# Pooled attention and a SiLU feed-forward on one core: attention of the next batch spread between the matmuls of each token tile

## The chip, the cores and the metric

The kernel runs on one core of one Trainium2 chip. The metric is the device time of one execution in microseconds (us); lower is better. The core has a matrix engine (PE, with its weight loads as PEld), a vector engine (DVE), ScalarE (ACT), GpSimd (POOL) and SyncE (SP); SP and POOL issue the DMAs of this kernel. SBUF is the on-chip memory, PSUM the memory that PE writes, used here in banks of 512 float32 columns.

## The reference

```python
def _attn_ref(q, k, v):                      # 8 batches, 8 heads, 576 positions, head dim 64
    pool = 8
    scale = 1.0 / np.sqrt(D)
    k_p = k.reshape(B, H, Sp, pool, D).mean(axis=3)       # Sp = 72
    v_p = v.reshape(B, H, Sp, pool, D).mean(axis=3)
    scores = scale * np.matmul(q, k_p.transpose(0, 1, 3, 2))
    scores = scores - np.max(scores, axis=-1, keepdims=True)
    attn = np.exp(scores)
    attn = attn / (np.sum(attn, axis=-1, keepdims=True) + 1e-09)
    return np.matmul(attn, v_p)

x = attn_out.transpose(0, 2, 1, 3).reshape(B * S, H * D)  # 4608 tokens x 512
h = x @ w_in                                              # 512 x 2048
g = h * (1.0 / (1.0 + np.exp(-h)))
out = g @ w_out                                           # 2048 x 512
```

Inputs and output are float32. Keys and values are averaged in groups of eight, so each query looks at 72 keys. A batch holds 576 tokens; 4608 tokens are nine tiles of 512.

## The kernel before, in words

The order of the instructions on each engine is made by a scheduler from the program, which is written as two loops one after the other.

**Attention** (`attn_head_pair`, 32 calls, one for each two heads of a batch). SP loads k and v of one head at a time (L121, L123, 144 KB each) into the tile `kvraw`, of which there are six. DVE adds up the groups of eight (L125, L130), makes a bf16 copy of v with a 65th column that holds 8.0 (L134, L135). PE transposes the pooled keys (L139) and the queries (L157, L160), which POOL loads with a cast to bf16 (L147, L151); ScalarE copies both out of PSUM (L141, L163). For each head PE makes the scores in a chunk of 512 and one of 64 queries (`sc_ps`, L170), ScalarE takes the exponential (`esT`, L177), PE multiplies by the values (`nu_ps`, L181: 64 rows of numerators, and the denominator as the 65th), ScalarE copies the result out (`numer_sb`, L184). SP writes the numerators to `x_pre_T` in HBM, transposed, and POOL writes the denominators to `denom_buf` (L186, L190).

**Feed-forward** (`moe_token_tile`, nine calls, one for each 512 tokens). SP reads `x_sb` (512 features x 512 tokens) and the denominators back (L200, L203). DVE takes the reciprocal (L205), POOL casts it (L207), PE spreads it to 64 rows for each head by a matmul with a table of zeros and ones (`rb_ps`, four for each tile, L211), and DVE multiplies x by it (L212). Then the "up" half: 16 groups of 4 matmuls of 512 columns into `hp_ps` (L218), each group followed by a Silu on ScalarE into `h_T` (L224). Then the "down" half: 4 groups of 16 matmuls into `o_ps` (L230), each copied out by ScalarE (L237) and stored by SP (L238). One tile has 128 of these large matmuls.

The weights `w_in` and `w_out` are loaded at the start by POOL with a cast to bf16, in one DMA each (L105, L107), ahead of its first load of q.

Of the kernel before, what the change touches and what calls it, by code (L numbers as in the profile page):

```python
# [27 lines left out]
FP32 = mybir.dt.float32  # L28
# [8 lines left out]
def kernel(  # L37
# [9 lines left out]
    nc = tc.nc  # L47
# [3 lines left out]
    Sp = S // POOL  # L51
    BH = B * H
# [3 lines left out]
    assert H % 2 == 0  # L56

    score_scale = float(1.0 / (D ** 0.5) / POOL)

    x_pre_T = nc.dram_tensor("x_pre_T", (d_model, NTOK), BF16, kind="Internal").ap()  # L60
    denom_d = nc.dram_tensor("denom_buf", (H, NTOK), BF16, kind="Internal").ap()

    k_pool = k.rearrange("b h (sp p) d -> b h sp p d", p=POOL)
    v_pool = v.rearrange("b h (sp p) d -> b h sp p d", p=POOL)

    S_CHUNKS = []
    s0 = 0
    while s0 < S:
        sl = min(512, S - s0)
        S_CHUNKS.append((s0, sl))  # L70
        s0 += sl
    QN = (S + 127) // 128
    NQ_FULL = QN - 1
    TL = S - 128 * NQ_FULL

# [3 lines left out]
    NT = NTOK // NTT  # L79

    w_in_r = moe_w_in.rearrange("(kt kp) f -> kp kt f", kp=128)
    w_out_r = moe_w_out.rearrange("(kt kp) d -> kp kt d", kp=128)
    xpt_r = x_pre_T.rearrange("(kt kp) t -> kp kt t", kp=128)

    singles = ctx.enter_context(tc.tile_pool(name="singles", bufs=1))
    ident = singles.tile([128, 128], FP32)
    make_identity(nc, ident)
    ident_bf = singles.tile([128, 128], BF16)
    nc.gpsimd.tensor_copy(out=ident_bf, in_=ident)

    trans_f = singles.tile([H, KF, 128], FP32, name="trans_f", bufs=1)
    nc.gpsimd.memset(trans_f, 1.0)
    nc.gpsimd.affine_select(
        out=trans_f, in_=trans_f, compare_op=ALU.is_ge, fill=0.0,
        base=0, channel_multiplier=-64, pattern=[[128, KF], [1, 128]],
    )
    nc.gpsimd.affine_select(
        out=trans_f, in_=trans_f, compare_op=ALU.is_ge, fill=0.0,
        base=63, channel_multiplier=64, pattern=[[-128, KF], [-1, 128]],
    )  # L100
    trans = singles.tile([H, KF, 128], BF16, name="trans", bufs=1)
    nc.gpsimd.tensor_copy(out=trans, in_=trans_f)

    w_in_sb = singles.tile([128, KF, d_ff], BF16)
    nc.gpsimd.dma_start(out=w_in_sb, in_=w_in_r)  # L105
    w_out_sb = singles.tile([128, KG, d_model], BF16)
    nc.gpsimd.dma_start(out=w_out_sb, in_=w_out_r)  # L107

    pools = {}

    def attn_head_pair(j):
        pa, pb, ps = pools["pa"], pools["pb"], pools["ps"]
        b = (2 * j) // H
# [168 lines left out]
```

## Time and profile before

| what | value |
|---|---|
| runs | 478.78, 475.38, 478.78 us; median 478.78 |
| profiled execution: span of the core | 476.0 us |
| busy in the span: PE, PEld, DVE, ACT, POOL | 374.4, 161.7, 189.2, 218.3, 127.2 us |
| instructions | 5267 |
| HBM read, written | 41.49 MB, 14.23 MB |
| DMA queues: issued by SP (hardware), by POOL (software) | 37.84 MB, 9.00 MB |

The profile is of one execution. Its span runs from the first to the last instruction, and is the profiled execution's own time; the runs were timed apart from it. In the rows of groups stand: line, engine, operation, output and inputs by the names of the program, shapes, count, then busy time and the mean duration of one in ns, then the idle time of the engine just before them and what ended it. In the timeline rows stand start (us), length (us), engine, line and operation; several of one kind in a row are merged ("x14"), and the length runs from the start of the first to the end of the last. Matmuls are pipelined: the length of one is longer than the distance to the next. In the rows by window stand the window, its length, then busy time and count for PE, PEld, DVE, ACT and POOL, the granted PE clock, the busy share of the DMA engines, and GB/s.

### The profile page before, as it was taken

The numbers are of one execution on the slowest core, as the hardware profiler recorded it, in microseconds if no ns is written. First come the engines' busy times: TensorE is split into PE (matmuls) and PEld (weight loads), VectorE is DVE, ScalarE is ACT, GpSimd is POOL, SyncE is SP. The second block draws the span as 40 slices with busy tenths as digits, with TensorE's granted clock in tenths as the row PEclk, the third lists the DMA queues.
The fourth block names the chain that finished last, engine by engine and source line by source line (L and its number), as shares of the span: only waits on it lengthen the run. The fifth ranks groups of instructions, "written<-read, shape, count | busy, mean of one in ns | idle before, by whom it ended". The sixth has DMA issues, their size and how long they took to land.

```text
span 476.0 us, 5267 instructions
## 1 busy us (share of the span) xinstructions
PE 374.4 (79%) x1612; PEld 161.7 (34%) x1636; DVE 189.2 (40%) x301; ACT 218.3 (46%) x502; POOL 127.2 (27%) x214
## 2 busy tenths in 40 slices
PE   0003777687777655379999999999999999999996
PEld 0001333233233321124444343443434434344342
DVE  5598766667766778999000202002020020200200
ACT  1002768778777665335162451623416244172441
POOL 7004878898699711210000000000000000000000
PEclk9999999999999999999999999999999999999999
DMA  7999999999999944321102112021120210201101
GB/s 174 239 228 199 155 146 158 157 172 162 157 158 176 162 147 136 84 81 44 67 22 90 44 44 90 1 90 44 49 85 0 90 44 14 75 0 45 45 22 67
DMA packets 69533, 47.18 MB, mean 99 GB/s; under 512 B 44344, under 2 KB 55168, under 8 KB 69504
## 3 DMA queue, kind: packets, MB, share of 16 engines
q1 hardware_dynamic: 25952, 37.84, 25.3%
q0 software_dynamic: 43552, 9.00, 21.0%
q8 instruction: 13, 0.21, 0.2%
q14 instruction: 16, 0.13, 0.1%
HBM read 41.49 MB, written 14.23 MB: 117 GB/s over the span
## 4 chain that ended last, share of the span: by engine, by line
PE 60%; DMA 17%; POOL 11%; issue 6%; ACT 3%; DVE 3%; SPq 0%; POOLq 0%; ACTq 0%
PE hp_ps L218 27%; PE o_ps L230 26%; DMA q_full<-in_q_dram 13%; POOL q_full L147 4%; POOL q_tail L151 3%; POOL denom_buf L190 3%; PE nu_ps L181 2%; PE rb_ps L211 2%; PE sc_ps L170 1%; ACT numer_sb L184 1%; DMA q_tail<-in_q_dram 1%; ACT esT L177 1%; DMA v_raw<-in_v_dram 1%; DMA x_sb<-x_pre_T 1%; PE qT_ps L157 1%
## 5 line engine op out<-in xcount | busy, mean ns | idle before, releaser
L218 PE MATMUL hp_ps<-x_sb,w_in_sb 128*128 128x512 bf16 x564 | 128.8, 384 | 1.7 <-ACT h_T L224 0.6
L230 PE MATMUL o_ps<-w_out_sb,h_T 128*128 128x512 bf16 x564 | 125.0, 379 | 0.6
L224 ACT ACTIVATE h_T<-hp_ps 128x512 bf16<-128x512 f32 x144 | 83.9, 597 | 52.8 <-PE hp_ps L218 52.7
L212 DVE TENSOR_TENSOR x_sb<-x_sb,rb_ps 128x512 bf16<-128x512 bf16 x36 | 23.0, 678 | 200.9 <-PE rb_ps L211 199.6
L218 PEld LDWEIGHTS <-w_in_sb 128*128 128x128 bf16 x576 | 55.6, 99 | 78.1 <-issue 15.3
L230 PEld LDWEIGHTS <-h_T 128*128 128x128 bf16 x576 | 56.4, 98 | 68.0
L130 DVE TENSOR_REDUCE v_p<-v_raw 72x64 f32<-72x512 f32 x64 | 64.6, 1010 | 22.2 <-DMA v_raw<-in_v_dram 20.1
L125 DVE TENSOR_REDUCE k_p_pair<-k_raw 72x64 f32<-72x512 f32 x64 | 64.7, 1011 | 19.3 <-DMA k_raw<-in_k_dram 18.9
L237 ACT COPY o_sb<-o_ps 128x512 f32<-128x512 f32 x36 | 21.1, 586 | 103.5 <-PE o_ps L230 97.7
L184 ACT CAST numer_sb<-nu_ps 65x512 bf16<-65x512 f32 (+1 forms) x128 | 44.3, 396 | 27.8 <-PE nu_ps L181 27.4
L147 POOL DMA_DIRECT2D q_full<-in_q_dram x64 | 52.9, 827 | 13.7 <-DMA w_in_sb<-in_moe_w_in_dram 11.3
L181 PE MATMUL nu_ps<-esT,vp_aug 72*65 72x512 bf16 (+1 forms) x128 | 41.8, 429 | 18.1 <-ACT esT L177 17.7
L177 ACT ACTIVATE esT<-sc_ps 72x512 bf16<-72x512 f32 (+1 forms) x128 | 45.1, 402 | 7.8 <-PE sc_ps L170 5.8
L170 PE MATMUL sc_ps<-q_T,kpT 64*72 64x512 bf16 (+1 forms) x128 | 44.2, 447 | 3.2 <-ACT kpT L141 2.4
L139 PE MATMUL kpT_ps<-ident,k_p_pair 72*128 72x72 f32 x32 | 11.7, 364 | 41.9 <-DVE k_p_pair L125 41.2
L190 POOL DMA_DIRECT2D denom_buf<-numer_sb x64 | 33.5, 524 | 40.7 <-ACT numer_sb L184 34.4
L151 POOL DMA_DIRECT2D q_tail<-in_q_dram x64 | 36.3, 567 | 20.6 <-DMA w_out_sb<-in_moe_w_out_dram 19.4
L207 POOL CAST recip_bf<-recip 8x512 bf16<-8x512 f32 x9 | 5.4, 603 | 124.4 <-PE rb_ps L211 112.0
L157 PE MATMUL qT_ps<-ident_bf,q_full 128*128 128x128 bf16 x128 | 20.5, 303 | 21.2 <-DMA q_full<-in_q_dram 16.2
L205 DVE RECIPROCAL recip<-den_sb 8x512 f32<-8x512 bf16 x9 | 29.4, 3305 | 0.0
L163 ACT COPY q_T<-qT_ps 128x576 bf16<-128x576 bf16 x32 | 20.4, 638 | 12.9 <-PE qT_ps L160 12.8
L181 PEld LDWEIGHTS <-vp_aug 72*65 72x65 bf16 x128 | 16.9, 148 | 26.9 <-issue 24.0
(25 smaller groups left out, 90.2 us busy)
## 6 DMA issues: line engine op xcount, KB each, us to landing
k_raw<-in_k_dram SPq DMA_DIRECT2D x64, 144.0 KB
v_raw<-in_v_dram SPq DMA_DIRECT2D x64, 144.0 KB
out_dram<-o_sb SPq DMA_DIRECT2D x36, 256.0 KB
x_pre_T<-numer_sb SPq DMA_DIRECT2D x64, 72.0 KB
x_sb<-x_pre_T SPq DMA_DIRECT2D x9, 512.0 KB
q_full<-in_q_dram POOLq DMA_DIRECT2D x64, 64.0 KB, 3.7
w_in_sb<-in_moe_w_in_dram POOLq DMA_DIRECT2D x1, 2048.0 KB, 17.5
w_out_sb<-in_moe_w_out_dram POOLq DMA_DIRECT2D x1, 2048.0 KB, 36.2
```

Of the source, the lines that this page charges most:

```text
L125: nc.vector.reduce_sum(out=k_p_pair[:, i, :], in_=k_raw.rearrange("a b c -> a c b"), axis=AX,)
L130: nc.vector.reduce_sum(out=v_p, in_=v_raw.rearrange("a b c -> a c b"), axis=AX)
L147: nc.gpsimd.dma_start(out=q_full[:, :, i, :], in_=q[b, h, : 128 * NQ_FULL, :].rearrange("(n p) d -> p n d", p=128),)
L151: nc.gpsimd.dma_start(out=q_tail[:TL, i, :], in_=q[b, h, 128 * NQ_FULL :, :],)
L170: nc.tensor.matmul(sc_ps[:, :sl], kpT[i * D : (i + 1) * D, :], q_T[i * D : (i + 1) * D, s0 : s0 + sl], start=True, stop=True,)
L177: nc.scalar.activation(esT[:, :sl], sc_ps[:, :sl], func=AF.Exp, scale=score_scale)
L181: nc.tensor.matmul(nu_ps[:, :sl], vp_augs[i], esT[:, :sl], start=True, stop=True)
L184: nc.scalar.copy(numer_sb[:, s0 : s0 + sl], nu_ps[:, :sl])
L190: nc.gpsimd.dma_start(out=denom_d[h : h + 1, tok0 : tok0 + S], in_=numer_sb[D : D + 1, :],)
L218: nc.tensor.matmul(hp_ps, w_in_sb[:, kk, gg * 128 : (gg + 1) * 128], x_sb[:, kk, :], start=(kk == 0), stop=(kk == KF - 1),)
L224: nc.scalar.activation(h_T[:, gg, :], hp_ps, func=AF.Silu)
L230: nc.tensor.matmul(o_ps, h_T[:, kk, mtok : mtok + 128], w_out_sb[:, kk, :], start=(kk == 0), stop=(kk == KG - 1),)
```

## The change

The kernel's body is written anew, and its order on each engine is the order in which it is written (`manual_schedule`); no scheduler moves anything.

- All of x, transposed, stays in SBUF (`xT`, 512 features x 4608 tokens, bf16). The tensors `x_pre_T` and `denom_buf` in HBM are gone, and so are `rb_ps` and its table.
- k, q and v of a whole batch come in one DMA each, all issued by SP in float32 (the first batch in two parts). POOL casts q to bf16; DVE pools k and v by three tensor-tensor additions each, in place of one reduction for each head.
- Two heads are worked on together. The scores of the two use the upper and the lower 64 rows of the PE array (`scores`), into two PSUM banks, and one Exp of 576 columns covers both. Denominators (against a block of ones that holds 8.0) and numerators of the two use the left and the right 64 columns (`values`), into one bank each. In the built program these matmuls have tiles of 64 x 128 and 128 x 64; all others have 128 x 128. Queries are taken in two halves of 288.
- 1/denominator is exp(-ln(denominator)) on ScalarE; DVE multiplies the numerators by it straight into `xT`. Ln and Exp lie in one activation table and Silu in another; the tables are loaded by hand, twice a tile.
- The batch a = t + 1 is worked on inside token tile t: `spread` calls a filler after a given matmul of the tile. In the up half: the loads of batch a + 1, the cast and the pooling, the transposes of k after matmul 22 and those of q after matmuls 26, 32, 38 and 44. In the down half: eight steps (four head pairs, two query halves), the scores after matmul 6n + 1 and the values after matmul 6n + 6. Batch 0 is worked on before the first tile; the last two tiles have no fillers.
- Large matmul outputs and transposes share three PSUM banks ("mm"). `o_ps` is copied out by DVE.
- The weights are loaded in four DMAs each, which POOL issues after its casts of the first q.

```diff
+    def load_batch(b, parts):
...
+        for i in range(parts):
+            hs = slice(i * hp, (i + 1) * hp)
+            nc.sync.dma_start(out=k_raw[:, hs, :], in_=k_src[:, hs, :])
+            nc.sync.dma_start(out=q_raw[:, hs, :], in_=q_src[:, hs, :])
+        for i in range(parts):
+            hs = slice(i * hp, (i + 1) * hp)
+            nc.sync.dma_start(out=v_raw[:, hs, :], in_=v_src[:, hs, :])
...
+    def pool_kv(b, which, parts):
...
+            w = POOL * D // 2
+            while w > D:
+                nc.vector.tensor_add(
+                    out=raw[:, hs, :w], in0=raw[:, hs, :w], in1=raw[:, hs, w : 2 * w]
+                )
+                w //= 2
+            nc.vector.tensor_add(
+                out=dst[:, hs, :], in0=raw[:, hs, :D], in1=raw[:, hs, D : 2 * D]
+            )
...
+    def q_transpose(b, p):
+        st = batches[b]
+        qT_ps = psum.tile([128, QJ, QP], BF16, tag="mm", bufs=3, name="qT_ps")
+        for j in range(QJ):
+            nc.tensor.transpose(
+                qT_ps[:, j, :],
+                st["q_bf"][:, p, j, :, :].rearrange("q s d -> q (s d)"),
+                ident[:QP, :QP],
+            )
+        qT = mid.tile([128, S], BF16, tag=f"qT{p}", bufs=1, name="qT")
+        nc.vector.tensor_copy(out=qT, in_=qT_ps.rearrange("d j q -> d (j q)"))
...
+    def scores(b, p, f):
+        st = batches[b]
+        cols = slice(f * HS, (f + 1) * HS)
+        sc_ps = psum.tile([SP, 2, 512], FP32, tag="sc", bufs=1, name="sc_ps")
+        for s in range(2):
+            rows = slice(s * D, (s + 1) * D)
+            nc.tensor.matmul(
+                sc_ps[:, s, :HS],
+                lhsT=st["kT"][rows, p, :],
+                rhs=st[f"qT{p}"][rows, cols],
+                start=True, stop=True,
+            )
+        es = mid.tile([SP, 2, HS], BF16, tag="es", bufs=3, name="es")
+        nc.scalar.activation(es, sc_ps[:, :, :HS], func=AF.Exp, scale=score_scale)
...
+    def values(b, p, f):
...
+        nu_ps = psum.tile([128, 512], FP32, tag="nd", bufs=3, name="nu_ps")
+        den_ps = psum.tile([128, 512], FP32, tag="nd", bufs=3, name="den_ps")
+        for s in range(2):
+            nc.tensor.matmul(
+                den_ps[s * D : (s + 1) * D, :HS],
+                lhsT=ones, rhs=es[:, s, :], start=True, stop=True,
+            )
+        for s in range(2):
+            nc.tensor.matmul(
+                nu_ps[s * D : (s + 1) * D, :HS],
+                lhsT=st["vp"][:, 2 * p + s, :], rhs=es[:, s, :],
+                start=True, stop=True,
+            )
+        lnd = mid.tile([128, HS], FP32, tag="lnd", name="lnd")
+        nc.scalar.activation(lnd, den_ps[:, :HS], func=AF.Ln)
+        rec = mid.tile([128, HS], FP32, tag="rec", name="rec")
+        nc.scalar.activation(rec, lnd, func=AF.Exp, scale=-1.0)
...
+    def spread(fillers, n):
+        todo = sorted(fillers, key=lambda f: f[0])
+        for i in range(n):
+            yield i
+            while todo and todo[0][0] <= i:
+                todo.pop(0)[1]()
...
+    for t in range(NT):
+        a = t + 1
+        f_up, f_down = [], []
+        if a < B:
+            if a + 1 < B:
+                f_up.append((0, lambda: load_batch(a + 1, 1)))
+            f_up.append((0, lambda: cast_q(a, 1)))
+            f_up.append((0, lambda: pool_kv(a, "k", 1)))
+            f_up.append((22, lambda: k_transpose(a)))
+            for p in range(NP):
+                f_up.append((26 + 6 * p, lambda p=p: q_transpose(a, p)))
+            f_up.append((50, lambda: pool_kv(a, "v", 1)))
+            f_down.append((0, attn_tables))
+            for n, (p, f) in enumerate(seq):
+                f_down.append((6 * n + 1, lambda p=p, f=f: scores(a, p, f)))
+                f_down.append((6 * n + 6, lambda p=p, f=f: values(a, p, f)))
+        moe_tables()
+        h_T = up(t, f_up)
+        down(t, h_T, f_down)
```

Where the instructions now stand, at three places. First, ScalarE between the last steps of attention and the first token tiles. Before, with `esT` the exponentials, `numer_sb` the copies out and `h_T` the Silus:

```order
L177 ACTIVATE esT<-sc_ps 72x64
L184 CAST numer_sb<-nu_ps 65x512
L184 CAST numer_sb<-nu_ps 65x64
L224 ACT_TABLE_LOAD
L224 ACTIVATE h_T<-hp_ps 128x512 x16
L237 COPY o_sb<-o_ps 128x512 x4
```
After, in each filled tile (`es` the exponentials, `lnd` and `rec` the two halves of the reciprocal):

```order
L211 ACT_TABLE_LOAD
L237 ACTIVATE h_T<-hp_ps 128x512 x16
L208 ACT_TABLE_LOAD
L177 ACTIVATE es<-sc_ps 72x576
L197 ACTIVATE lnd<-den_ps 128x288
L199 ACTIVATE rec<-lnd 128x288
```
The last three stand eight times in a row before the next table load; the copies of `o_ps` are no longer on this engine, and the tables change twice a tile.

Second, PE among the large matmuls. Before, where the down half of one tile ends and the next tile begins:

```order
L230 LDWEIGHTS h_T
L230 MATMUL o_ps<-w_out_sb,h_T 128x512
L211 LDWEIGHTS trans
L211 MATMUL rb_ps<-recip_bf,trans 128x512
...
L218 LDWEIGHTS w_in_sb
L218 MATMUL hp_ps<-x_sb,w_in_sb 128x512
```
After, in the first step of a down half (`sc_ps` the scores, `den_ps` and `nu_ps` denominators and numerators; rows that only repeat are left out at the dots):

```order
L250 MATMUL o_ps<-w_out_sb,h_T 128x512
L170 LDWEIGHTS kT
L170 MATMUL sc_ps<-qT,kT 72x288
...
L250 MATMUL o_ps<-w_out_sb,h_T 128x512
L186 LDWEIGHTS ones
L186 MATMUL den_ps<-es,ones 64x288
...
L191 LDWEIGHTS vp
L191 MATMUL nu_ps<-es,vp 64x288
...
L250 LDWEIGHTS h_T
L250 MATMUL o_ps<-w_out_sb,h_T 128x512
```
Scores and values have moved from a stage of their own to between the large matmuls.

Third, POOL at the start of the program. Before:

```order
L105 DMA w_in_sb<-in_moe_w_in_dram 128x4x2048
L102 CAST trans<-trans_f 8x512
L107 DMA w_out_sb<-in_moe_w_out_dram 128x16x512
L147 DMA q_full<-in_q_dram 128x4x64
L151 DMA q_tail<-in_q_dram 64x64
```
After:

```order
masks.py:199 AFFINE_SELECT ident<-ident 128x128
L267 MEMSET ones 72x64
L113 CAST q_bf<-q_raw 96x6x64 x8
L272 DMA w_in_sb<-in_moe_w_in_dram 128x4x512 x4
L275 DMA w_out_sb<-in_moe_w_out_dram 128x4x512 x4
L113 CAST q_bf<-q_raw 96x6x64 x56
```
The eight casts of the first q, which wait for its load, now stand ahead of the weights.

More of the change, by code (lines that the diff above doesn't have):

```diff
@@ L55 @@
     d_ff = moe_w_in.shape[1]
[L56 to L74, printed above, removed]
+    NP = H // 2
     KF = d_model // 128
@@ L195, in moe_token_tile @@
[L195 to L216 removed]
+    big = ctx.enter_context(tc.tile_pool(name="big", bufs=2))
```

263 lines of the change are left out of this document (126 added, 137 removed).

## Prediction

> **What bounds the kernel now.** I read the slices first, then the chain of waits, then busy time by stage.
>
> ```profile
> PE   0003777687777655379999999999999999999996
> ACT  1002768778777665335162451623416244172441
> PEclk9999999999999999999999999999999999999999
> DMA  7999999999999944321102112021120210201101
> PE 60%; DMA 17%; POOL 11%; issue 6%; ACT 3%; DVE 3%; SPq 0%; POOLq 0%; ACTq 0%
> ```
> ```profile
> 0.00:198.00 198.00, 111.26 (x448) 47.21 (x449) 142.33 (x258) 112.00 (x321) 122.32 (x206) 1.00 0.91 166
> 198.00:476.00 278.00, 263.15 (x1164) 114.53 (x1187) 46.83 (x44) 106.32 (x181) 4.83 (x8) 1.00 0.15 52
> ```
> There are two programs, one after the other. For 198 us (busy columns: PE, PEld, DVE, ACT, POOL) attention runs, its DMA engines full (share 0.91) and PE busy 111 of 198 us. Then for 278 us the token tiles run on PE alone, with DMA at 0.15. Neither uses what the other needs; the chain has DMA and POOL steps in the first part and little but matmuls in the second.
>
> The second part's rate, from the output copies (one per 16 matmuls, four per tile):
>
> ```profile
> 254.66 0.59 ACT L237 COPY o_sb<-o_ps 128x512 f32<-128x512 f32 x1 [2.90 <-PE o_ps L230]
> 258.12 0.59 ACT L237 COPY o_sb<-o_ps 128x512 f32<-128x512 f32 x1 [2.87 <-PE o_ps L230]
> 284.29 0.59 ACT L237 COPY o_sb<-o_ps 128x512 f32<-128x512 f32 x1 [2.90 <-PE o_ps L230]
> 472.37 0.59 ACT L237 COPY o_sb<-o_ps 128x512 f32<-128x512 f32 x1 [2.87 <-PE o_ps L230]
> ```
> A 512-column matmul takes 3.46/16 = 0.216 us. A tile takes 284.29 − 254.66 = 29.6 us; its 128 matmuls are 27.65, so some 2.0 belong to the four rb_ps broadcasts and their wait. The last copy starts 3.6 us before the end of the span (476.0).
>
> PE has a second speed, which the granted clock (9 throughout) does not show:
>
> ```profile
> 206.04 0.15 PEld L218 LDWEIGHTS <-w_in_sb 128*128 128x128 bf16 x1 [0.28 <-issue]
> 206.47 0.15 PEld L218 LDWEIGHTS <-w_in_sb 128*128 128x128 bf16 x1 [0.28 <-issue]
> 209.88 0.15 PEld L218 LDWEIGHTS <-w_in_sb 128*128 128x128 bf16 x1 [0.28 <-issue]
> L170 PE MATMUL sc_ps<-q_T,kpT 64*72 64x512 bf16 x64 | 40.8, 637 | 3.2 <-ACT kpT L141 2.4 <-ACT q_T L163 0.7
> L218 PE MATMUL hp_ps<-x_sb,w_in_sb 128*128 128x512 bf16 x564 | 128.8, 384 | 1.7 <-ACT h_T L224 0.6 <-DMA x_sb<-x_pre_T 0.3 <-issue 0.2
> ```
> The first token-tile matmuls come 0.43 us apart until 209.88, about 10 of them, and only then 0.216. All of attention runs at the slow rate (637 ns for 512 columns against 384).
>
> **The change, part by part.** *Removed:* the attention stage as a stage of its own, the rb_ps broadcasts (9 × 2.0 = 18 us), and the trip of x through HBM. Floor: nine tiles of 27.65 = 248.8 us. All that is added has to be paid per tile, at the start, or at the end.
>
> *Up half of a tile (seven tiles have attention to fill in).* 64 matmuls are 13.8 us. Between them stand 28 transposes, 4 of k and 24 of q:
>
> ```profile
> 86.58 0.58 PE L157 MATMUL qT_ps<-ident_bf,q_full 128*128 128x128 bf16 x4 [2.11 <-DMA q_full<-in_q_dram]
> L157 PE MATMUL qT_ps<-ident_bf,q_full 128*128 128x128 bf16 x128 | 20.5, 303 | 21.2 <-DMA q_full<-in_q_dram 16.2 <-DMA q_tail<-in_q_dram 2.9 <-DMA denom_buf<-numer_sb 2.0
> 6.50 0.35 PE L139 MATMUL kpT_ps<-ident,k_p_pair 72*128 72x72 f32 x1 [6.50 <-DVE k_p_pair L125]
> 6.89 0.22 ACT L141 CAST kpT<-kpT_ps 128x72 bf16<-128x72 f32 x1 [4.80 <-PE kpT_ps L139]
> L212 DVE TENSOR_TENSOR x_sb<-x_sb,rb_ps 128x512 bf16<-128x512 bf16 x36 | 23.0, 678 | 200.9 <-PE rb_ps L211 199.6 <-DMA x_sb<-x_pre_T 0.5
> L224 ACT ACTIVATE h_T<-hp_ps 128x512 bf16<-128x512 f32 x144 | 83.9, 597 | 52.8 <-PE hp_ps L218 52.7
> L207 POOL CAST recip_bf<-recip 8x512 bf16<-8x512 f32 x9 | 5.4, 603 | 124.4 <-PE rb_ps L211 112.0 <-DVE recip L205 12.3
> ```
> Four take 0.58 us, the last of them 0.3, so about 0.1 each at the slow rate; 96 columns at 0.216 per 512 would be 0.04. I take 0.08: 2.2 us (1.1 to 3.0). Stalls: DVE copies the last o_sb (0.68 by the tensor-tensor row), then pools k, 3584 elements a partition, 4.7 us at 678/512; so kp stands ready 5.6 us into the tile, and its transposes are due after 23 matmuls, 5.0. The transposes also take turns in the three "mm" banks: twice a bank comes back after four matmuls (0.86) while the Silu needs 1.03 (0.38 to the matmul's end, 0.6 for itself, and 0.05 for the hand-over, as from 6.85 to 6.89). Together 0.8. The eight q casts (0.5 each by POOL's 603 ns for 512) run in the tile before and hide; pooling v has some 3 us of slack. Up half: 16.8 us.
>
> *Down half.* 64 matmuls, 13.8, and eight steps, one after every six matmuls: two score matmuls, two for den_ps, two for nu_ps, each 288 columns, 0.121 us by 0.216 × 288/512. No row shows two half-array matmuls in different halves. Bounds for a pair: 0.12 (wholly side by side) and 0.24 (in turn). I take the middle, 0.18, since the second has its own weights to load; 0.54 a step. Going between full and part-array tiles costs something:
>
> ```profile
> 266.88 0.38 PE L211 MATMUL rb_ps<-recip_bf,trans 8*128 8x512 bf16 x1
> 267.19 1.47 PE L218 MATMUL hp_ps<-x_sb,w_in_sb 128*128 128x512 bf16 x6
> ```
> rb_ps contracts 8 rows on a part-array tile. From it to the next full matmul are 0.31 us, where 512 columns take 0.216: 0.095 for one switch. A step has four (in and out for the scores, in and out for den and nu): 0.38. The Trainium skill (TensorEngine Tiling (Array Packing), Key Properties) says that a change of tiling mode drains the array and that tiles in one mode run in parallel; the row bears out the first, and no run here shows the second. By that page a pair would be 0.12 and the total some 10 us lower.
>
> So PE's step is 6 × 0.216 + 0.54 + 0.38 = 2.22 us. ScalarE must keep up:
>
> ```profile
> L177 ACT ACTIVATE esT<-sc_ps 72x512 bf16<-72x512 f32 x64 | 38.0, 593 | 7.8 <-PE sc_ps L170 5.8 <-PE qT_ps L160 1.7 <-PE qT_ps L157 0.3
> L177 ACT ACTIVATE esT<-sc_ps 72x64 bf16<-72x64 f32 x64 | 13.4, 210 | 0.0
> L163 ACT COPY q_T<-qT_ps 128x576 bf16<-128x576 bf16 x32 | 20.4, 638 | 12.9 <-PE qT_ps L160 12.8
> 210.40 1.28 ACT L224 ACT_TABLE_LOAD   x1 [13.78 <-PE hp_ps L218]
> 211.69 2.55 ACT L224 ACTIVATE h_T<-hp_ps 128x512 bf16<-128x512 f32 x5
> ```
> 288 columns: 210 + 224 × 0.855 = 0.40 us for Ln; for the second Exp, whose input is in SBUF, no row exists, 0.43 (0.40 to 0.60). The 576-column Exp is 0.64, of which 0.1 overlaps (five of 0.6 take 2.55). The loop den, Ln, Exp, next es, next den: 0.35 (a pair, and 0.384 − 0.216 of latency) + 0.40 + 0.48 + 0.54 + 0.05 = 1.8 us, under PE's 2.22: hidden, with 0.4 to spare. If PE were faster than that, this loop would set the step. Only the first step shows ScalarE: the last Silu ends 0.8 after the up half, the table load takes 1.28, the first Exp 0.64, so den can start at 2.75 against PE's 2.0: 0.75. The Trainium skill (ScalarE: Activation LUTs, What ACT_TABLE_LOAD costs) adds a drain of about 1.4 to each load; here the next instruction starts at 211.69, right at the load's end, and by the page the total would be 10 us higher. The load back to Silu comes 15 matmuls early and hides.
>
> Down half: 13.8 + 8 × 0.92 + 0.75 = 21.9. A filled tile: 38.7; seven: 271. Two plain ones: 55.3.
>
> *The start.* Batch 0's attention stands alone ahead of the tiles.
>
> ```profile
> 0.81 0.43 SPq L121 DMA_DIRECT2D k_raw<-in_k_dram  x1
> 3.27 1.01 DVE L125 TENSOR_REDUCE k_p_pair<-k_raw 72x64 f32<-72x512 f32 x1 [2.30 <-DMA k_raw<-in_k_dram]
> 2.00:3.00 1.00, 0.00 (x0) 0.00 (x0) 0.00 (x0) 0.09 (x1) 1.00 (x3) 1.00 0.68 244
> 24.00:36.00 12.00, 0.70 (x2) 0.36 (x2) 11.68 (x22) 0.44 (x2) 0.00 (x0) 1.00 1.03 227
> w_in_sb<-in_moe_w_in_dram POOLq DMA_DIRECT2D x1, 2048.0 KB, 17.5
> w_out_sb<-in_moe_w_out_dram POOLq DMA_DIRECT2D x1, 2048.0 KB, 36.2
> 3.16 0.89 POOL L105 DMA_DIRECT2D w_in_sb<-in_moe_w_in_dram  x1
> 4.60 1.16 POOL L107 DMA_DIRECT2D w_out_sb<-in_moe_w_out_dram  x1
> ```
> A batch is 3 × 8 × 576 × 64 × 4 bytes = 3.54 MB. Six transfers of 0.59 MB at SP's 244 GB/s are 2.4 us each, k, q, k, q, v, v: the first half of v lands at about 14.4 and is pooled by 16.7. Then eight steps at ScalarE's 1.4 to 1.6 us: the first tile starts at about 29 us (25 to 34). Its first ten matmuls run at the slow rate: 2.1.
>
> The weights now stand behind the casts of q on POOL: issued at about 14 us, not 3.2. Before, both had landed at 4.6 + 36.2 = 40.8, after 37.6 us beside k and v. After 14 + 37.6 = 51.6 the last quarter of w_out is there; the 13th down matmul asks for it at 29 + 2.1 + 16.8 + 2.6 = 50.5. I put 2 us. Upper bound: SP queues batches 1 and 2 at once; 7.1 MB and 4.2 MB of weights at 240 GB/s end at 61: 10.5 us.
>
> *Later transfers:* 3.5 MB in and 1 MB out per 38 us tile are 120 GB/s of the 227 shown, two batches ahead: hidden. *The end:* 3.7.
>
> **Sum**, against the profiled span: 29 + 2.1 + 2 + 271 + 55.3 + 3.7 = 363 us. The runs lie between 0.6 under and 2.8 over that span, the median 2.8 over; I add 1: **364 us**.
>
> **Rivals.** *The pairs do not overlap* (the change does not do what it says): 3 × 0.06 × 56 steps, +10: 374. Nothing in the profile speaks for or against. *Every half-array matmul exposes its weight load:* six of 0.121 + 0.095 and two switches back are 1.49 a step for 0.92, +32: 396. For it: after rb_ps the load was exposed; against: in one mode loads lie under matmuls. *The weights come late:* +9: 373. *Switches hide as well and ScalarE's loop sets the step at 1.8:* −0.42 × 56, −24: 340. *PE stays at the slow rate:* in the first 198 us PE was busy more than half the time and never sped up, so filled tiles full of short gaps might not either. Each matmul then costs 0.211 more; it is slower than before from 114/0.211 = 540 of the 1152 matmuls, that is, if both halves of the filled tiles run so; all seven give 7 × 128 × 0.211 = 189 more: 553. Against it: tiles with rb_ps pauses of half a microsecond kept 0.216. The Trainium skill (TensorE: Matmul & The Clock Gate, Part 1) has the array fall back to half clock only after a whole idle window of about 3.4 us; by it this does not come.
>
> **How the numbers follow.** Forecast 0.53 (its own terms give 350 to 378), pairs in turn 0.15, weight loads exposed 0.10, weights late 0.10, ScalarE's loop 0.08, slow PE 0.04. The range 338 to 392 holds all but the exposed loads and the slow PE, 0.86. About 1% (5 us) can be told from no change. Faster by more: all but the slow PE, 0.95; that one with only part of the tiles slow could end near 478: 0.01; slower 0.04.
>
> **What would show it.** Right: PE's row of slices at 9 from about the third slice to the end; output copies some 38 to 39 us apart from tile to tile for seven tiles, then 27.65; matmuls at 384 ns; the first hp_ps at 25 to 34 us; two sc_ps matmuls less than 0.1 us apart; den_ps waiting for es only in each tile's first step. Wrong: filled tiles over 42 us or under 35; hp_ps or o_ps at 600 ns in the middle of the run; o_ps waiting for w_out in the first tile by more than 10 us; ScalarE named as the releaser of den_ps in every step.

## The result

The changed kernel takes 363.75 us (median of 4 runs, 362.77 to 364.9) and the kernel before 478.78 us. The ratio is 0.762, with a 95% interval of 0.7585 to 0.765. The profiled execution has a span of 360.9 us; the sum of the prediction was 363. Of the runs of the kernels tried below, a single one (1739 us, of six of the kernel with all three edits) is left out of its figures; what slowed it is not known.

### The profile after

First the slices and the chain, as they were read before:

```profile
PE   0378855799999999999999999999999999999995
...
PEclk9999985699999999999999999999999999999999
...
PE 76%; DMA 16%; ACT 4%; POOL 2%; SPq 0%; issue 0%; DVE 0%
```
PE stands at 9 from the ninth slice to the last but one: from there on the matmuls set the time, and attention and transfers run beside them (ACT is busy 139.97 of 218.35 us in the third window below, the DMA share is 0.44). One piece does not fit. In slices 6 to 8 (45 to 72 us) PE is at 5, 5 and 7 and the granted clock at 8, 5 and 6, and of the 16% of DMA in the chain 12 belong to w_out. That is the first tile's down half.

The span cut at the first matmul of the tiles, at the end of the first tile, and behind the last filled tile (window, length, then busy time and count of PE, PEld, DVE, ACT, POOL; granted clock, DMA share, GB/s):

```profile
0.00:28.75 28.75, 11.79 (x76) 5.66 (x76) 18.15 (x24) 11.34 (x24) 10.68 (x23) 1.00 0.96 230
28.75:83.45 54.70, 42.39 (x206) 16.04 (x205) 22.87 (x24) 25.56 (x45) 8.33 (x16) 0.84 0.66 165
83.45:301.80 218.35, 213.65 (x1226) 89.66 (x1225) 129.27 (x138) 139.97 (x252) 19.14 (x40) 1.00 0.44 111
301.80:360.90 59.10, 55.38 (x257) 24.89 (x255) 6.22 (x9) 20.39 (x33) 0.00 (x0) 1.00 0.10 40
```
The start takes 28.75 us (29 in the sum), six filled tiles 218.35, 36.39 each (38.7 in the sum), two plain tiles and the end 59.1 (55.3 + 3.7). The first tile takes 54.7 where the sum has 38.7 + 2.1 + 2 = 42.8. So two terms are off, in opposite directions: +11.9 in the first tile, −13.9 in the six tiles behind it. What remains is −2.

A filled tile, the one from 156 us, on PE. Its up half, with the 28 transposes between the 64 matmuls:

```profile
156.23 5.13 PE L230 MATMUL hp_ps<-xT,w_in_sb 128*128 128x512 bf16 x23
161.35 0.30 PE L142 MATMUL kT_ps<-ident,kp 72*128 72x72 bf16 x4
161.48 1.03 PE L230 MATMUL hp_ps<-xT,w_in_sb 128*128 128x512 bf16 x4
162.35 0.42 PE L155 MATMUL qT_ps<-ident,q_bf 96*128 96x96 bf16 x6
162.61 1.46 PE L230 MATMUL hp_ps<-xT,w_in_sb 128*128 128x512 bf16 x6
```
From start to start the four transposes of k take 0.13 us and six of q 0.26: 0.03 to 0.04 each, 1.2 in all, and no row has a wait. The half lasts 15.1 us. Its down half:

```profile
171.37 0.59 PE L250 MATMUL o_ps<-w_out_sb,h_T 128*128 128x512 bf16 x2
...
174.18 0.31 PE L186 MATMUL den_ps<-es,ones 72*64 72x288 bf16 x2 [0.78 <-ACT es L177]
...
176.29 0.31 PE L186 MATMUL den_ps<-es,ones 72*64 72x288 bf16 x2
176.44 0.29 PE L191 MATMUL nu_ps<-es,vp 72*64 72x288 bf16 x2
176.66 0.39 PE L250 MATMUL o_ps<-w_out_sb,h_T 128*128 128x512 bf16 x1
...
178.41 0.31 PE L186 MATMUL den_ps<-es,ones 72*64 72x288 bf16 x2
```
Only the first den_ps waits for ScalarE (0.78 us). After that a step is 2.12 us from den_ps to den_ps: 1.30 for six o_ps matmuls and 0.82 for the attention pairs and the changes of tile shape around them. A whole pair ("x2") lasts 0.29 to 0.31, hardly longer than one such matmul would (an estimate: 0.12 for 288 columns, and the 0.16 by which a 512-column row, 0.38, exceeds its distance to the next, 0.216), and nu_ps starts 0.15 after den_ps.

The first tile's longest wait, from the waits between 28 and 85 us (total, times, longest):

```profile
PE o_ps L250 <- DMA w_out_sb<-in_moe_w_out_dram: 10.8, 4, 3.3
```
And of the page the row of POOL's queue (packets, MB, share of 16 engines) and the sum of the traffic; then the issues of w_out (durations in ns, first and last start) and the time from each to its landing:

```profile
q0 software_dynamic: 4224, 4.19, 6.9%
...
HBM read 36.70 MB, written 9.44 MB: 128 GB/s over the span
```
```profile
L275 POOL DMA_DIRECT2D w_out_sb<-in_moe_w_out_dram x4: 790/804/817, 18.3 to 20.4; - x4
...
DMA to landing us min/median/max: 32.0/38.1/44.9
```
o_ps waits for quarters of w_out that are issued at 18.3 to 20.4 us and land 32 to 45 us later, the last at 20.4 + 44.9 = 65.3. The queue's row and the sum hold something that the prediction had overlooked. Queue q0 carries the weights and counts 4.19 MB, as they are written into SBUF. But eight batches of q, k and v are 28.3 MB of the 36.70 read; the other 8.4 MB are the weights, float32 in HBM and cast on the way. The transfer is twice as large on its reading side as its own rows say. What that costs is less sure: by the queues' shares (6.9% for 4.19 MB here, 38.6% for 37.75 MB on SP's queue) a megabyte as written took the DMA engines 1.6 times as long as one of SP's.

The waits have a price beyond themselves: the matmuls behind each are slow again. A row behind one wait, and the window around it:

```profile
54.77 1.44 PE L250 MATMUL o_ps<-w_out_sb,h_T 128*128 128x512 bf16 x3 [3.10 <-DMA w_out_sb<-in_moe_w_out_dram]
```
```profile
54.00:63.00 9.00, 4.85 (x14) 1.34 (x14) 1.11 (x1) 1.50 (x3) 3.66 (x8) 0.50 0.85 213
```
Three o_ps last 1.44 us, and the granted clock of the window is 0.50.

### The profile page after: what moved, and what is told of

It reads as the page before. It is cut to its first block, busy times and chain, and to the rows that moved or that the text cites. A ratio compares the mean times of both kernels' runs of the same rounds, so it can differ in the third digit from the quotient of the medians.

```text
span 360.9 us, 4481 instructions
## 1 busy us (share of the span) xinstructions
PE 323.2 (90%) x1760; PEld 136.3 (38%) x1760; DVE 176.5 (49%) x194; ACT 197.2 (55%) x353; POOL 38.1 (11%) x79
## 3 DMA queue, kind: packets, MB, share of 16 engines
q1 hardware_dynamic: 20904, 37.75, 38.6%
q0 software_dynamic: 4224, 4.19, 6.9%
HBM read 36.70 MB, written 9.44 MB: 128 GB/s over the span
## 4 chain that ended last, share of the span: by engine, by line
PE 76%; DMA 16%; ACT 4%; POOL 2%; SPq 0%; issue 0%; DVE 0%
PE o_ps L250 35%; PE hp_ps L230 31%; DMA w_out_sb<-in_moe_w_out_dram 12%; PE den_ps L186 4%; PE sc_ps L170 3%; DMA q_raw<-in_q_dram 3%; ACT L208 2%; PE nu_ps L191 2%; PE qT_ps L155 2%; ACT es L177 1%; ACT h_T L237 1%; POOL w_in_sb L272 1%; POOL w_out_sb L275 1%; POOL q_bf L113 1%; PE kT_ps L142 0%
## 5 line engine op out<-in xcount | busy, mean ns | idle before, releaser
L250 PE MATMUL o_ps<-w_out_sb,h_T 128*128 128x512 bf16 x576 | 148.4, 387 | 10.8 <-DMA w_out_sb<-in_moe_w_out_dram 10.8
L230 PE MATMUL hp_ps<-xT,w_in_sb 128*128 128x512 bf16 x576 | 134.5, 385 | 1.5 <-DMA w_in_sb<-in_moe_w_in_dram 1.0
L201 DVE TENSOR_TENSOR xT<-nu_ps,rec 128x288 bf16<-128x288 f32 x64 | 71.4, 1124 | 77.3 <-ACT rec L199 77.2
L230 PEld LDWEIGHTS <-w_in_sb 128*128 128x128 bf16 x576 | 54.7, 99 | 64.0 <-issue 4.4
L257 DVE COPY o_sb<-o_ps 128x512 f32<-128x512 f32 x36 | 27.1, 752 | 59.8 <-PE o_ps L250 59.7
L113 POOL CAST q_bf<-q_raw 96x384 bf16<-96x384 f32 x64 | 31.3, 533 | 211.1 <-DMA q_raw<-in_q_dram 178.7
L197 ACT ACTIVATE lnd<-den_ps 128x288 f32<-128x288 f32 x64 | 26.2, 409 | 49.8 <-PE den_ps L186 49.8
L177 ACT ACTIVATE es<-sc_ps 72x576 bf16<-72x576 f32 x64 | 40.4, 631 | 17.2 <-PE sc_ps L170 17.1
L130 DVE TENSOR_TENSOR k_raw<-k_raw 72x1024 f32<-72x1024 f32 (+2 forms) x18 | 28.4, 1579 | 9.0 <-DMA k_raw<-in_k_dram 8.7
L199 ACT ACTIVATE rec<-lnd 128x288 f32<-128x288 f32 x64 | 28.3, 443 | 2.4 <-DVE xT L201 0.4
L161 DVE COPY qT<-qT_ps 128x576 bf16<-128x576 bf16 x32 | 14.6, 457 | 29.1 <-PE qT_ps L155 29.1
L130 DVE TENSOR_TENSOR v_raw<-v_raw 72x1024 f32<-72x1024 f32 (+2 forms) x18 | 28.3, 1572 | 0.4
L191 PE MATMUL nu_ps<-es,vp 72*64 72x288 bf16 x128 | 20.4, 310 | 1.7 <-DVE vp L134 0.9
## 6 DMA issues: line engine op xcount, KB each, us to landing
w_out_sb<-in_moe_w_out_dram POOLq DMA_DIRECT2D x4, 512.0 KB, 38.1
```

The source lines that it names most:

```text
L113: nc.gpsimd.tensor_copy(out=q_bf[:, p, :, s, :], in_=st["q_raw"][:, 2 * p + s, :].rearrange("q (j d) -> q j d", d=D),)
L130: nc.vector.tensor_add(out=raw[:, hs, :w], in0=raw[:, hs, :w], in1=raw[:, hs, w : 2 * w])
L177: nc.scalar.activation(es, sc_ps[:, :, :HS], func=AF.Exp, scale=score_scale)
L191: nc.tensor.matmul(nu_ps[s * D : (s + 1) * D, :HS], lhsT=st["vp"][:, 2 * p + s, :], rhs=es[:, s, :], start=True, stop=True,)
L199: nc.scalar.activation(rec, lnd, func=AF.Exp, scale=-1.0)
L201: nc.vector.tensor_mul(out=dst[:, f * HJ : (f + 1) * HJ, :], in0=nu_ps[:, :HS].rearrange("d (j q) -> d j q", q=QP), in1=rec.rearrange("d ( ...
```

## The experiments

Theory after the result: the mechanism of the prediction holds (PE bound, pairs side by side, ScalarE hidden), the transposes and pairs are cheaper than put, and the late weights cost about 15 us instead of 2. The rivals are named with each experiment; the one to the whole is that the terms of the sum were right and the first tile long for another reason, such as batch 1's attention finding less cover there. Each part was tried by itself; in the first two experiments the first tile, with the same attention in it, takes 39.2 and 39.3 us in place of 54.7, so that rival falls. The start of all kernels with the same program up to the first tile lies between 28.75 and 31.9 us in their profiles, so small differences are read from the distance between tiles, not from the total.

### What the late weights cost: issued first

```
-    cast_q(0, 2)
     NC = 4
     for c in range(NC):
         cs = slice(c * d_ff // NC, (c + 1) * d_ff // NC)
         nc.gpsimd.dma_start(out=w_in_sb[:, :, cs], in_=w_in_r[:, :, cs])
     for c in range(NC):
         cs = slice(c * KG // NC, (c + 1) * KG // NC)
         nc.gpsimd.dma_start(out=w_out_sb[:, cs, :], in_=w_out_r[:, cs, :])
+    cast_q(0, 2)
```

> The changed kernel with one edit: the eight weight transfers are issued on POOL ahead of the casts of batch 0's q, at about 3 us, not behind them at 15 to 21. Theory A: the late issue is not what makes the weights late. The weights are read as float32, 8.4 MB, and with batches 0, 1 and 2 (10.6 MB) 19 MB have to come in before the last quarter of w_out is there, in whatever order they are issued; 65 us at the 290 GB/s that the changed kernel read. Then the weights share the DMA engines with batch 0, the first hp_ps comes at 38 to 46 us, not 28.75, the o_ps no longer wait for w_out, and the time stays within 6 us of 363.8: 358 to 370. Theory B, the prediction's words: the weights are late because they stand behind the casts. Then the first hp_ps stays near 29 to 32 and 8 us or more of the 10.8 us that o_ps waits for w_out go: 350 to 356.

Measured: 353.8 us, ratio 0.7385 [0.7358, 0.7411]. The first matmul of its tiles, and its transfers of w_out from issue to landing:

```profile
35.13 1.06 PE L230 MATMUL hp_ps<-xT,w_in_sb 128*128 128x512 bf16 x2 [0.33 <-issue]
```
```profile
DMA to landing us min/median/max: 30.5/37.5/45.2
```
Neither theory is right as written. The weights take as long from issue to landing as in the changed kernel (37.5 us for 38.1 in the median), so, issued at 4.5 us, they come 13 to 14 us earlier, and no o_ps waits for them. The first batch loses some of that: the first tile begins at 35.13. Its last copy stands at 74.51 in place of 83.65. Theory A failed where it put all three batches ahead of the last weights: POOL's queue runs beside SP's, and when the last weights are there (6.7 + 45.2 = 51.9 us) SP's has brought 8.2 of the 10.6 MB; the end of batch 2 comes behind them. Theory B had the total right and the start wrong.

### What the late weights cost: batch 2 out of their way

```
-                f_up.append((0, lambda: load_batch(a + 1, 1)))
+                f_down.append((17, lambda: load_batch(a + 1, 1)))
```

> The changed kernel with one edit: the loads of the batch after next are issued not at the start of a tile's up half but in its down half, behind the first output store (place 17 of 64), so that batch 2's 3.5 MB don't run beside the weights. Theory A (the DMA engines are full until 65 us, and batch 2's bytes are what the weights wait behind): 15.5 MB are left before the last quarter of w_out, at 290 GB/s 53 us; the wait of o_ps for w_out falls from 10.8 us to 0 to 4, and the slow matmuls that follow each such wait go with it: 349 to 355. Rival B (the weights' queue runs at a pace of its own, some 75 to 115 GB/s as written, whatever stands beside it): the last w_out lands at 60 or later as now, and the time stays at 360 to 365. Rival C (loads at that place come too late for the next tile, whose kT_ps then waits for k): later filled tiles grow from 36.4 us to over 38, and the time is over 370.

Measured: 353.19 us, ratio 0.7372 [0.7347, 0.7397]. Its issues of w_out, the time to their landing, and the wait that is left in the first tile:

```profile
L275 POOL DMA_DIRECT2D w_out_sb<-in_moe_w_out_dram x4: 790/804/817, 20.2 to 22.4; - x4
...
DMA to landing us min/median/max: 26.7/29.4/32.1
```
```profile
PE o_ps L250 <- DMA w_out_sb<-in_moe_w_out_dram: 0.8, 1, 0.8
```
Theory A. With batch 2's 3.5 MB away, the quarters of w_out land after 29.4 us in the median in place of 38.1, and the 10.8 us of waiting become 0.8. From the first weight's issue (17.2 us here, 15.2 in the changed kernel) to the last landing it is 37.3 us in place of 50.1, with 3.8 MB on SP's queue beside it in place of 7.4. Rival B falls: the same queue is faster when less runs beside it. Rival C falls too, but has a grain of truth: the later tiles take 36.76 us, 0.37 more than in the changed kernel (more on this below).

### Pairs: side by side or in turn

```
-        for s in range(2):
+        for s in (0, 1, 0, 1):
             nc.tensor.matmul(
                 den_ps[s * D : (s + 1) * D, :HS],
                 lhsT=ones, rhs=es[:, s, :], start=True, stop=True,
             )
```

> The changed kernel with one addition: the pair of den_ps matmuls is issued twice, each time from zero, so that the values stay what they are. 64 pairs more, 56 of them in filled tiles, without any further change of tile shape. Theory A (the two halves of a pair run side by side): 0.12 to 0.15 us a pair in the filled tiles, 7 to 8 us: 370 to 372, the steady step 2.24 to 2.27 us. Rival B (in turn): 0.24, 13.6 us: 377 to 378. Rival C (each half-array matmul exposes its weight load as well): 0.4 a pair or more, over 22 us: 386 or more.

Measured: 370.05 us, ratio 0.7707 [0.7686, 0.7728]. A step of it:

```profile
186.37 0.44 PE L186 MATMUL den_ps<-es,ones 72*64 72x288 bf16 x4
186.63 0.29 PE L191 MATMUL nu_ps<-es,vp 72*64 72x288 bf16 x2
```
Four den_ps take 0.26 us to the start of nu_ps where two took 0.15, and the filled tile grows from 36.39 to 37.37: 0.98 / 8 = 0.12 a pair, the time of one matmul of 288 columns (0.121). Theory A; "in turn" and "exposed weight load" fall.

### The changes of tile shape

```
-                f_down.append((6 * n + 1, lambda p=p, f=f: scores(a, p, f)))
+                f_down.append((max(1, 6 * n), lambda p=p, f=f: scores(a, p, f)))
```

> The changed kernel with one edit: the score matmuls of step n+1 stand right behind the nu_ps of step n, where one full-array matmul stood between. A step goes from four changes between full and part-array tiles to three (o_ps to den, nu to sc, sc to o_ps). Theory A (each change costs 0.095 to 0.115 us, also the one from 72x64 to 64x72 tiles): 49 steps, 4.7 to 5.6 us less: 358 to 359, the steady step 2.00 to 2.02 us in place of 2.12. Rival B (only a change between full and part-array tiles costs, the one between two part-array shapes is free): twice that, 9.3 to 11 us: 353 to 354.5, step 1.90. Rival C (what shows as the cost of a change is the exposed weight load of a pair, which stays): no difference, 363 to 364.5.

Measured: 358.65 us, ratio 0.749 [0.7469, 0.7511]. A step of it:

```profile
183.52 0.31 PE L186 MATMUL den_ps<-es,ones 72*64 72x288 bf16 x2
183.66 0.29 PE L191 MATMUL nu_ps<-es,vp 72*64 72x288 bf16 x2
183.88 0.31 PE L170 MATMUL sc_ps<-qT,kT 64*72 64x288 bf16 x2
...
185.53 0.31 PE L186 MATMUL den_ps<-es,ones 72*64 72x288 bf16 x2
```
The step is 2.01 us for 2.12, the tile 35.64 for 36.39: 0.75 / 7 = 0.107 for each change saved. Theory A. The change from nu_ps to sc_ps, between two part-array shapes, costs as much as one to the full array (0.22 from the start of nu_ps to that of sc_ps, as to o_ps in the changed kernel).

### The first step

```
-                f_down.append((6 * n + 1, lambda p=p, f=f: scores(a, p, f)))
-                f_down.append((6 * n + 6, lambda p=p, f=f: values(a, p, f)))
+                f_down.append((6 * n + 5 if n else 1, lambda p=p, f=f: scores(a, p, f)))
+                f_down.append((6 * n + 10, lambda p=p, f=f: values(a, p, f)))
```

> The changed kernel with one edit: all attention work of the down half but the first scores stands four full-array matmuls later (values at place 10 of 64, not 6; the last at 52). Theory A (the first step's 0.78 us is the table load and the first Exp, which four matmuls, 0.86 us, cover): den_ps no longer waits for es, and 7 x 0.78 = 5.5 us go: 357.5 to 359; the filled tile takes 35.6 us in place of 36.4. Rival B (ScalarE's chain at the end of the tile, Ln, Exp, the product on DVE and the load of Silu's table, now comes late for the next tile's first hp_ps): what is won in front is lost behind, 362 to 366, with hp_ps waiting for xT.

Measured: 359.52 us, ratio 0.7505 [0.7481, 0.7529], with the first tile starting 3 us later in its profile. The first den_ps of a tile, and the last copies of two tiles:

```profile
174.41 0.31 PE L186 MATMUL den_ps<-es,ones 72*64 72x288 bf16 x2
```
```profile
156.64 0.69 DVE L257 COPY o_sb<-o_ps 128x512 f32<-128x512 f32 x1 [0.56 <-PE o_ps L250]
...
192.18 0.69 DVE L257 COPY o_sb<-o_ps 128x512 f32<-128x512 f32 x1 [0.56 <-PE o_ps L250]
```
den_ps waits no more, and the tile is 35.54 for 36.39: 0.85, slightly more than the 0.78 of the wait. Nothing is given back at the end of the tile, so theory A; that the total lies half a microsecond above its range may go with the late start (the first tile's last copy is 1.9 us later than in the changed kernel), which is not shown.

### ScalarE's loop

```
-                f_down.append((6 * n + 1, lambda p=p, f=f: scores(a, p, f)))
-                f_down.append((6 * n + 6, lambda p=p, f=f: values(a, p, f)))
+                f_down.append((4 * n + 3 if n else 1, lambda p=p, f=f: scores(a, p, f)))
+                f_down.append((4 * n + 6, lambda p=p, f=f: values(a, p, f)))
```

> The changed kernel with one edit: a step of attention after every four full-array matmuls, not six, the first where it was. PE's own step is then 4 x 0.216 + 0.82 = 1.69 us. Theory A (ScalarE's loop of Ln, Exp, next es and hand-overs takes 1.8 us, as predicted): seven steps a tile wait 0.1 to 0.15, and the tile grows by 0.7 to 1.1 us: 368 to 372; den_ps waits for es in every step. Rival B (the loop takes 2.0 or more): 2.2 us a tile or more, 379 or more. Rival C (the loop is under 1.69): no difference, 363 to 364.5.

Measured: 370.1 us, ratio 0.7707 [0.7683, 0.7731]. A step of it on PE, with the exponential on ScalarE that its last row needs:

```profile
184.86 0.31 PE L186 MATMUL den_ps<-es,ones 72*64 72x288 bf16 x2
...
185.79 0.82 PE L250 MATMUL o_ps<-w_out_sb,h_T 128*128 128x512 bf16 x3
186.00 0.63 ACT L177 ACTIVATE es<-sc_ps 72x576 bf16<-72x576 f32 x1
186.68 0.31 PE L186 MATMUL den_ps<-es,ones 72*64 72x288 bf16 x2
```
The step is 1.82 us where PE needs 1.69, and the tile grows by 0.95 us: theory A, the loop takes 1.82. With a step after every six matmuls 0.3 us of cover is left. PE's rows name no wait here, but the last o_ps starts at 186.22 by its pitch and den_ps 0.46 later, where 0.32 is usual, and 0.05 after the end of es (186.00 + 0.63). The other rival for the step, DVE's product of the step before, had started at 184.30 and taken 1.12, so it was long done.

### What the spreading itself brings

```
-            f_up.append((22, lambda: k_transpose(a)))
-            for p in range(NP):
-                f_up.append((26 + 6 * p, lambda p=p: q_transpose(a, p)))
...
-            f_down.append((0, attn_tables))
-            for n, (p, f) in enumerate(seq):
-                f_down.append((6 * n + 1, lambda p=p, f=f: scores(a, p, f)))
-                f_down.append((6 * n + 6, lambda p=p, f=f: values(a, p, f)))
...
         down(t, h_T, f_down)
+        if a < B:
+            attn_tables()
+            k_transpose(a)
+            for p in range(NP):
+                q_transpose(a, p)
+            for n, (p, f) in enumerate(seq):
+                scores(a, p, f)
+                if n:
+                    values(a, *seq[n - 1])
+            values(a, *seq[-1])
```

> The changed kernel with the spreading undone: the loads, the casts of q and the sums of k and v stay where they are, but the transposes and the eight steps of the next batch run as one piece behind each tile's down half. It tells what of the 115 us the order between the matmuls brings, and what x in SBUF, the missing broadcasts and the hidden loads bring. Theory A (the spreading carries about half): batch 0 alone shows 2.3 us from the transposes to the first scores and 1.30 a step, set by ScalarE and DVE; with a table load of 1.28, the tail of 1.6 and ten slow matmuls behind, 16 to 18 us a batch on top of 27.65, where a filled tile takes 36.4: seven times 7.5 to 9.5, 416 to 430. Rival B (it carries little, since PE has to do the same matmuls anyway): up to 3 us a tile, 364 to 385. Beside it: whether PE falls to the slow rate in each such piece (sc_ps pairs 0.24 apart from den_ps, not 0.15), as it was in all of batch 0's attention.

Measured: 417.62 us, ratio 0.8695 [0.8666, 0.8724], 52 us more than with the spreading by the ratios, 54 by the medians; its tiles are 42.6 to 44.2 us apart. Part of such a piece on PE, and the windows over it:

```profile
171.13 0.31 PE L170 MATMUL sc_ps<-qT,kT 64*72 64x288 bf16 x2 [0.74 <-ACT es L177]
171.37 0.31 PE L186 MATMUL den_ps<-es,ones 72*64 72x288 bf16 x2
...
175.41 0.45 PE L186 MATMUL den_ps<-es,ones 72*64 72x288 bf16 x2 [0.16 <-DVE xT L201]
```
```profile
168.50:171.90 3.40, 2.17 (x32) 1.47 (x30) 2.29 (x6) 1.07 (x2) 1.63 (x4) 1.00 0.48 125
171.90:175.30 3.40, 2.05 (x14) 1.11 (x14) 2.19 (x2) 3.30 (x9) 2.03 (x5) 0.84 0.93 231
...
172.00:184.60 12.60, 9.64 (x47) 3.98 (x47) 10.39 (x9) 11.25 (x25) 1.93 (x5) 0.59 0.91 209
```
Theory A. ACT is busy 3.30 of 3.40 us of the second window: ScalarE sets the pace. PE loses its fast rate in the piece: a pair goes from 0.31 to 0.45 long, the granted clock from 1.00 to 0.84 and to 0.59 over the rest. Of the 115 us that the change brings, somewhat under half comes from the spreading, and some 62 us from all else together (x kept in SBUF, no broadcasts, batches loaded ahead).

### All three edits, and where the 0.37 us went

> The changed kernel with three edits at once: loads of the batch after next behind the first output store of the down half, the steps four matmuls later, and the scores right behind the values of the step before. Theory A (the three costs are separate: late weights, first step, one change of tile shape a step): the single gains add up, about 10 + 5.5 + 5 us: 340 to 347. Rival B (with the step nearer to ScalarE's loop of 1.8, or with the loads late for the next tile, part is given back): 348 to 356.

It joins the edits of the three kernels above (loads at place 17 of the down half; scores at 6 * n + 4, the first at 1; values at 6 * n + 10). Measured: 341.97 us, ratio 0.711 [0.7088, 0.7132], theory A. The late loads keep their price here too, and the next kernel takes it away by leaving only batch 2 late:

```
-                f_down.append((17, lambda: load_batch(a + 1, 1)))
+                (f_up if t else f_down).append((0 if t else 17, lambda: load_batch(a + 1, 1)))
```

> The kernel with all three edits, but only batch 2's loads stand in the down half; those of the later batches are back at the start of the up half. In the kernels with late loads each later tile takes 0.37 us more before kT_ps, which waits for kp: POOL's casts of q then run beside DVE's sums of k, which take 3.72 + 0.87 us there and 3.53 + 0.69 with POOL idle. Theory A (DVE is slowed by POOL's casts beside it): with q's casts back in the tile before, kT_ps no longer waits, the sums take 3.53 and 0.69 again, and the filled tile falls from 35.16 to 34.8: 2 us in all, 339 to 341 (between 341.97 and 363.75, the casts are the only thing moved). Rival B (the sums are slowed by the late transfers into SBUF, or kp is late for another reason): no difference, 341.5 to 343.

Measured: 340.2 us, ratio 0.7091 [0.707, 0.7112]. First DVE's sums of k and POOL's casts of q in the kernel with all loads late, then the same two in this one:

```profile
107.46 3.72 DVE L130 TENSOR_TENSOR k_raw<-k_raw 72x2048 f32<-72x2048 f32 x2
111.21 0.87 DVE L134 TENSOR_TENSOR kp<-k_raw 72x512 bf16<-72x512 f32 x1
```
```profile
107.44 7.26 POOL L113 CAST q_bf<-q_raw 96x384 bf16<-96x384 f32 x8 [28.35 <-DMA q_raw<-in_q_dram]
```
```profile
106.03 3.53 DVE L130 TENSOR_TENSOR k_raw<-k_raw 72x2048 f32<-72x2048 f32 x2
109.59 0.69 DVE L134 TENSOR_TENSOR kp<-k_raw 72x512 bf16<-72x512 f32 x1
```
```profile
121.39 3.67 POOL L113 CAST q_bf<-q_raw 96x384 bf16<-96x384 f32 x8 [26.53 <-DMA q_raw<-in_q_dram]
```
Side by side the casts take 7.26 us and the sums 0.37 more; apart they take 3.67 and 4.22. From the third tile on kT_ps no longer waits for kp, and the tile falls from 35.16 to 34.78; the gain is read from the tiles, since the intervals of the two totals overlap. Theory A; rival B falls, since transfers run beside the sums at as much as 191 GB/s here, too (140.8 to 145.1 us), with 190 in the kernel with all loads late (107.4 to 112.1 us). The Trainium skill (SBUF — State Buffer, Who interferes with whom) has VectorE instructions with two SBUF inputs and GpSimd's reads take turns at one port; the casts, longer by most of the sums' time, agree with it.

The last kernel issues w_in, besides, between the two parts of the casts of batch 0's q (`cast_q` calls load_w_in, which holds the loop taken out here, behind its first part):

```
-    cast_q(0, 2)
     NC = 4
-    for c in range(NC):
-        cs = slice(c * d_ff // NC, (c + 1) * d_ff // NC)
-        nc.gpsimd.dma_start(out=w_in_sb[:, :, cs], in_=w_in_r[:, :, cs])
...
+    cast_q(0, 2, (load_w_in,))
```

> The kernel before it in this list with one more edit: the four transfers of w_in are issued on POOL between the two parts of the casts of batch 0's q, some 5 us earlier, w_out behind them as before. Theory A (the weights share the DMA engines about evenly with SP's loads, so that whatever they gain the first batch loses): the first hp_ps comes 1 to 3 us later, o_ps waits 1 to 3 us less for w_out, and the time stays within 1.5 us of the kernel without the edit, 338 to 342. Rival B (an earlier issue brings the weights at no cost to batch 0): the first hp_ps stays where it is, the 2.6 us that o_ps waits go, 336 to 338.

Measured: 338.73 us, ratio 0.7074 [0.7051, 0.7096]; the intervals of the last two overlap, so a gain is not shown. The 2.3 us that o_ps waited for w_out are gone; the first hp_ps is at 31.25 for 29.51, as theory A had it, but that lies within the spread of the starts. So what the first batch lost by it, and with that the choice between the theories, stays open. It is the fastest version tried, 7% under the changed kernel.

## Why the prediction was right, and which of its terms were not

- *What bounds it*: right. PE is busy 35.6 of the 36.39 us of a filled tile (213.65 of 218.35 over six).
- *Up half, 16.8*: 15.1 measured. The transposes are 1.2 for 2.2, since the price came from rows at the slow rate, and the lower bound of 1.1 was nearly the truth. The stalls of 0.8 do not come: kp is ready in time, because DVE's sums take 4.2 and not 4.7 us. There is no slack, though: in the kernels with late loads 0.37 us of delay showed in full as a wait.
- *Pairs, 0.18*: 0.12 (twice den_ps). The lower bound was right, as the Trainium skill's page on tiles had it (TensorEngine Tiling (Array Packing), Key Properties). *Changes of shape, 0.095*: 0.107 by the saved one. The two errors cancel in part: the step is 2.12 for 2.22.
- *First step, 0.75*: 0.78, and 0.85 came back when it was covered. The first Exp starts where the table load ends, as the prediction read it; the drain that the Trainium skill (ScalarE: Activation LUTs, What ACT_TABLE_LOAD costs) adds is not there, behind the load or ahead of it (the last Silu starts at 171.57 and lasts 0.60):

```profile
172.19 1.28 ACT L208 ACT_TABLE_LOAD   x1
173.48 0.65 ACT L177 ACTIVATE es<-sc_ps 72x576 bf16<-72x576 f32 x1
```
- *ScalarE's loop of 1.8, hidden*: 1.82, hidden.
- *The start, 29, and ten slow matmuls, 2.1*: 28.75, where kernels with the same start have up to 31.9, so the close agreement is in part luck. The slow matmuls come 0.43 apart, as put, but there are twelve, 2.6 us: three, then nine of the next twenty, whose length of 6.40 is 1.9 more than at full rate. The wait between them, 0.5, was not in the sum:

```profile
28.75 1.46 PE L230 MATMUL hp_ps<-xT,w_in_sb 128*128 128x512 bf16 x3
30.71 6.40 PE L230 MATMUL hp_ps<-xT,w_in_sb 128*128 128x512 bf16 x20 [0.49 <-DVE xT L201]
```
- *Weights, 2 us (upper bound 10.5)*: this step failed. Beyond a filled tile of 36.39 and the slow matmuls and the wait for xT at its head (2.6 and 0.5), the first tile takes 54.7 − 36.39 − 3.1 = 15.2 us: 10.8 of waits for w_out, 1.0 for w_in, and the slow matmuls behind each, which were not in the step at all. The 2 us took over the 37.6 us that the weights had needed in the kernel before, from the first issue to the last landing, where SP's queue brought 4.0 MB beside them. Here it brings 7.4, since batch 2's loads run at the same time, and the same way takes 50.1 (15.2 to 65.3 us, where the step had 14 to 51.6); without batch 2 it takes 37.3. So the time was taken over as if no more than before would run beside the weights. The upper bound did count batch 2, but the weights as they are written, 4.2 MB, which gave 61 us; with the 8.4 that are read it would have been 14 + (7.1 + 8.4) / 0.24 = 79. The last landing, 65.3, lies between the two. Getting the weights early or batch 2 out of the way returns about 10 us of the total in either case.
- *The rival "weights late"* is in effect what happened, and the prediction's own sign against itself, o_ps waiting for w_out by more than 10 us, came true (10.8). It does not show in the total, because seven filled tiles were 2.3 us cheaper each: −16.2, against +13.2 for the weights, 0.5 for two more slow matmuls and 0.5 for the wait for xT, is the −2 between sum and span. That the forecast of 364 met 363.75 so closely is luck: errors of opposite sign cancelled.
- *The rival "PE stays slow"* falls for the filled tiles, where PE is busy 98% of the time. In attention by itself it comes about, with gaps of no more than 0.74 us; whether a filled tile with as many gaps would lose it was not tried.

## What to carry to other kernels

Before a transfer's time is taken over from another kernel, ask what will run beside it until it lands, and read the size of a transfer that casts from what HBM reads as well, not only from what the issue row or the queue writes. Here small matmuls put between large ones cost PE only their columns, once for a pair in two halves of the array, plus about 0.11 us for every change of tile shape: group equal shapes, and leave the other engines' loop a little more room than it needs (0.3 us of 2.12 here). A total that agrees proves no term; compare the stages.

## What the hardware showed that was not expected

- PE loses its full clock without any long pause. In attention by itself it is busy 2.17 and 2.05 of 3.40 us, its longest gap is 0.74 us, and the granted clock goes from 1.00 to 0.59. The Trainium skill (TensorE: Matmul & The Clock Gate, Part 1) puts the fall down to a whole idle window of some 3.4 us, and names frequent short pauses as a second way, without a figure; here some 1.3 us in each 3.4, in pieces, were enough.
- The granted clock in the rows shows this here, and did not show the slow matmuls before the first tile (1.00 in the first 28.75 us, with pairs 0.45 long).
- DVE's product of nu_ps and rec, 288 columns written with a step of six, takes 1124 ns, where a bf16 copy of 576 columns (qT, L161) takes 457; whether the step, the two float32 inputs or something else makes it was not tried:

```profile
L201 DVE TENSOR_TENSOR xT<-nu_ps,rec 128x288 bf16<-128x288 f32 x64 | 71.4, 1124 | 77.3 <-ACT rec L199 77.2
```
In the filled tiles it hides; in attention by itself den_ps waits for it six times in each piece, 1.4 to 1.6 us together.
